# One softmax pass without the replication step, projections moved between attention blocks, and an output stage per chunk

## The chip, the cores and the metric

The kernel runs on one core of a Trainium2 chip. The metric is the device time of one execution in microseconds. Four runs of the kernel before took 351.17 to 352.73 us, with a median of 352.28 us. The profile is of one further execution, which took 352.67 us; its span, from the first to the last instruction, is 350.8 us.

## The reference

All tensors are bf16. `x` has S = 2048 rows of D = 512. Attention has 32 heads of 16 elements and a window of eight keys at distances 0, 2, ..., 14 (causal); the feed-forward part has 1792 inner columns.

```
xn  = layernorm(x)
q, k, v = split(xn @ wqkv)                      # 32 heads x 16
logit[h,s,w] = q[h,s] . k[h,s-2w] / 4           # w = 0..7, masked where s-2w < 0
o[h,s] = sum_w softmax_w(logit)[h,s,w] * v[h,s-2w]
s   = o @ wo
h   = gelu_tanh(xn @ w_gate) * (xn @ w_up)
g   = silu(h @ w_down)
out = x + s * g
```

## The kernel before

**Layout.** The sequence is worked on in four chunks of 512 columns (`CH`), and activations are transposed: a tile is 128 features by 512 positions. D is four blocks of 128 features (`NF`). `kT` and `vT` hold k and v of the whole sequence with 14 zero columns ahead, so that a window element is the same tile read `off` = 2w columns earlier. Products of positions with shifted positions are done on VectorE (`prod`, `avp`); TensorE sums them with constant matrices.

**Start (lines 65 to 146).** GpSimd and VectorE build constants: `ident`; `b56` (sums 16 rows of a head); `rep` and `summat`, each from 16 copies of 32x32 blocks on VectorE. SyncE loads `x` and `wqkv`, then the three feed-forward weights. ScalarE copies the v columns of `wqkv` into another order (`wvp`, line 122). Sixteen row tiles are normalised (VectorE and ScalarE) and transposed on TensorE into `xnT`.

**Per chunk (lines 163 to 290).** In program order:
- Projection: 12 groups of four matmuls give q, k (line 168) and v (line 181); ScalarE copies each out of PSUM (lines 177 and 187).
- Scores: 32 `prod` on VectorE (line 198) and 32 matmuls with a 128x32 stationary operand (line 202). Four window elements share one PSUM tile, each in its own 32 partitions (`L_lo`, `L_hi`).
- Softmax: two `Exp` (line 212), two `den_ps` matmuls with `summat`, `Ln` and `Exp` for the reciprocal `rden` (lines 223, 225). Eight `er_ps` matmuls with `rep` (line 229) spread each window element's 32 rows over 128, and ScalarE copies them to `erep` (line 233).
- Values: for each of four blocks, eight `avp` on VectorE (line 239), eight matmuls with `ident` into `acc` (line 243), and one product with `rden` into `oT_sb` (line 247).
- Feed-forward: for each of 14 inner blocks, eight matmuls into `g_ps` and `u_ps` (line 259); GELU by its sigmoid form in three ScalarE and three VectorE instructions (lines 266 to 277), giving `h_q`. Then for each of four row blocks 14 `dacc` matmuls (line 282), `sig` (line 287) and `g_t` (line 289); GpSimd writes `g_t` to DRAM (line 290).

**Final stage (lines 299 to 318),** after all chunks: for each of 16 row blocks four `s_ps` matmuls with `wo_sb` (line 305), a load of `g_t` back (GpSimd queue, line 311) and of `x` (SyncE queue, line 313), two VectorE products (lines 315, 317) and a store.

**Order.** A planner fixes one order for each engine ahead of the run. Mostly it is program order; an instruction whose inputs and buffers are planned to be ready is put ahead where an engine would stand idle. All PSUM tiles share one pool of eight banks. `prod` has eight buffers, `avp` four, `q_sb` two, and `h_q` one. ScalarE loads a function table where `Exp`, `Ln` or `Sigmoid` follows another of them (ACT_TABLE_LOAD).

Of the kernel before, what the change touches and what calls it, by code (L numbers as in the profile page):

```python
# [17 lines left out]
def kernel(  # L18
# [52 lines left out]
    b56f = consts.tile([P, 56], F32, name="b56f")  # L71
    nc.gpsimd.memset(b56f[:], 1.0)
    nc.gpsimd.affine_select(
        out=b56f[:], in_=b56f[:], compare_op=ALU.is_ge, fill=0.0,
        base=384, pattern=[[-16, 56]], channel_multiplier=1,
    )
    nc.gpsimd.affine_select(
        out=b56f[:], in_=b56f[:], compare_op=ALU.is_ge, fill=0.0,
        base=-369, pattern=[[16, 56]], channel_multiplier=-1,
    )  # L80
    b56 = consts.tile([P, 56], BF, name="b56")
    nc.gpsimd.tensor_copy(out=b56[:], in_=b56f[:])
    rep = consts.tile([P, 4, P], BF, name="rep")
    nc.gpsimd.memset(rep[:], 0.0)
    for wl in range(4):
        for dl in range(4):
            nc.vector.tensor_copy(
                out=rep[32 * wl:32 * wl + 32, wl, 32 * dl:32 * dl + 32],
                in_=ident[32 * wl:32 * wl + 32, 32 * wl:32 * wl + 32],
            )  # L90
    summat = consts.tile([P, P], BF, name="summat")
    for pb in range(4):
        for mb in range(4):
            nc.vector.tensor_copy(
                out=summat[32 * pb:32 * pb + 32, 32 * mb:32 * mb + 32],
                in_=ident[32 * pb:32 * pb + 32, 32 * pb:32 * pb + 32],
            )
    eps_t = consts.tile([P, 1], F32, name="eps_t")
# [11 lines left out]
    g_dram = dram.tile([S, D], BF, name="g_dram")  # L110
# [40 lines left out]
    nc.sync.dma_start(out=wd_sb[:], in_=B_w_down.rearrange("(k p) n -> p k n", p=P))  # L151
    QT = CH
    assert QT == 512 and NCK * CH == S
    with tc.tile_pool(name="prodp", bufs=8) as prodp, \
            tc.tile_pool(name="ep", bufs=2) as ep, \
# [3 lines left out]
            tc.tile_pool(name="hq", bufs=1) as hq, \  # L159
            tc.tile_pool(name="ffnp", bufs=2) as ffnp:  # L160
        for c in range(NCK):
            t0 = c * CH
            q_sb = qp.tile([P, NF, CH], BF, name="q_sb")
            for fq in range(2 * NF):
                col = fq * P
                ps = psum.tile([P, CH], F32, name="ps", tag="mm512")
                for kt in range(NKT):
                    nc.tensor.matmul(  # L168
                        ps[:], lhsT=wqkv_sb[:, kt, col:col + P],
                        rhs=xnT[:, kt, t0:t0 + CH],  # L170
                        start=(kt == 0), stop=(kt == NKT - 1),
                    )
                if fq < NF:
                    dst = q_sb[:, fq, :]
                else:
                    dst = kT[:, fq - NF, PAD + t0:PAD + t0 + CH]
                nc.scalar.activation(out=dst, in_=ps[:], func=ACT.Copy)  # L177
            for b in range(NF):
                psv = psum.tile([P, CH], F32, name="psv", tag="mm512")
                for kt in range(NKT):  # L180
                    nc.tensor.matmul(  # L181
                        psv[:], lhsT=wvp[:, kt, b * P:(b + 1) * P],
                        rhs=xnT[:, kt, t0:t0 + CH],
                        start=(kt == 0), stop=(kt == NKT - 1),
                    )
                dst = vT[:, b, PAD + t0:PAD + t0 + CH]
                nc.scalar.activation(out=dst, in_=psv[:], func=ACT.Copy)
# [31 lines left out]
            den_ps = psum.tile([P, CH], F32, name="den_ps", tag="mm512")
            nc.tensor.matmul(den_ps[:], lhsT=summat[:], rhs=e_lohi[0][:], start=True, stop=False)  # L220
            nc.tensor.matmul(den_ps[:], lhsT=summat[:], rhs=e_lohi[1][:], start=False, stop=True)
            lnd = work.tile([P, CH], F32, name="lnd", bufs=2)
            nc.scalar.activation(out=lnd[:], in_=den_ps[:], func=ACT.Ln)
            rden = work.tile([P, CH], F32, name="rden", bufs=2)
            nc.scalar.activation(out=rden[:], in_=lnd[:], func=ACT.Exp, scale=-1.0)
            erep = erepp.tile([P, W, CH], BF, name="erep")
            for w in range(W):
                er_ps = psum.tile([P, CH], F32, name="er_ps", tag="mm512")
                nc.tensor.matmul(  # L229
                    er_ps[:], lhsT=rep[:, w % 4, :], rhs=e_lohi[w // 4][:],  # L230
                    start=True, stop=True,
                )
                nc.scalar.activation(out=erep[:, w, :], in_=er_ps[:], func=ACT.Copy)  # L233
# [44 lines left out]
            for j in range(QT // P):  # L278
# [70 lines left out]
```

## Time and profile before

| what | value |
|---|---|
| median of four runs | 352.28 us |
| profiled execution: its time / its span | 352.67 us / 350.8 us |
| TensorE busy | 293.1 us (84%), 1288 matmuls |
| VectorE busy | 241.5 us (69%) |
| ScalarE busy | 195.4 us (56%) |
| GpSimd busy | 28.5 us (8%) |
| mean granted TensorE clock | 0.968 |

A busy TensorE in this table is not TensorE at its pace: a 128x512 matmul has a duration of 379 ns, but in an unbroken run the next one starts 216 ns after it, so that durations overlap. The pace is read from a run of many matmuls, less the last one's duration.

### The profile page before, as it was taken

What the parts mean: (1) busy time and instruction counts of PE and PEld (TensorE: products, weight loads), DVE (VectorE), ACT (ScalarE), POOL (GpSimd) and SP (SyncE); (2) the same over time, 40 slices, a digit from 0 to 9 for tenths busy, and PEclk for the clock granted to TensorE, in tenths of its full rate; (3) what the DMA queues carried; (4) which work ended last, traced back from release to release, by engine and by line L of the source; (5) the groups of instructions that cost most, each with busy time, mean ns of one, the idle gap of its engine ahead of it and who ended that gap; (6) DMA issues with size and microseconds to landing.
All of it is one profiled execution on the core that took longest, in us unless ns stands there. A gap on an engine that the chain in (4) does not pass through costs nothing.

```text
span 350.8 us, 3905 instructions
## 1 busy us (share of the span) xinstructions
PE 293.1 (84%) x1288; PEld 121.5 (35%) x1288; DVE 241.5 (69%) x584; ACT 195.4 (56%) x333; POOL 28.5 (8%) x69
## 2 busy tenths in 40 slices
PE   0239986999899959999899689998999599989940
PEld 0224321344344213444343224443432134434410
DVE  5971677989723959798328598995167698972764
ACT  2396663499526471897255817993465448962000
POOL 7400000000020000000110000000100100001430
PEclk9999998999999998999999989999999899999995
DMA  7992000000010000000000000000100300001685
GB/s 250 365 398 96 1 0 0 3 0 0 0 47 15 0 0 3 0 1 2 30 30 0 2 1 0 0 2 15 47 2 0 91 0 2 0 0 46 206 258 181
DMA packets 12180, 18.34 MB, mean 52 GB/s; under 512 B 1408, under 2 KB 9344, under 8 KB 12160
## 3 DMA queue, kind: packets, MB, share of 16 engines
q1 hardware_dynamic: 10112, 13.37, 10.9%
q0 software_dynamic: 2048, 4.72, 4.4%
q8 instruction: 10, 0.16, 0.2%
q14 instruction: 10, 0.08, 0.1%
HBM read 13.89 MB, written 4.19 MB: 52 GB/s over the span
## 4 chain that ended last, share of the span: by engine, by line
PE 40%; DVE 21%; issue 16%; ACT 11%; DMA 8%; POOL 1%; SPq 1%; DVEq 0%; POOLq 0%; ACTq 0%
PE ps L168 8%; DVE h_q L277 8%; PE dacc L282 7%; PE L_hi L202 5%; DVE gg_sb L276 4%; PE acc L243 4%; PE L_lo L202 4%; PE psv L181 4%; DMA wqkv_sb<-in_A_wqkv_dram 4%; DVE t_sb L270 4%; ACT sg_sb L274 3%; DVE avp L239 3%; DMA x_t<-in_A_x_dram 3%; PE g_ps L259 2%; PE er_ps L229 2%
## 5 line engine op out<-in xcount | busy, mean ns | idle before, releaser
L198 DVE TENSOR_TENSOR prod<-q_sb,kT 128x512 bf16<-128x512 bf16 x128 | 44.7, 418 | 29.0 <-ACT kT L177 23.4
L259 PE MATMUL u_ps<-xnT,wu_sb 128*128 128x512 bf16 x224 | 59.4, 379 | 0.0
L259 PE MATMUL g_ps<-xnT,wg_sb 128*128 128x512 bf16 x224 | 58.1, 379 | 0.0
L239 DVE TENSOR_TENSOR avp<-erep,vT 128x512 bf16<-128x512 bf16 x128 | 45.7, 417 | 17.6 <-ACT erep L233 17.1
L243 PE MATMUL acc<-avp,ident 128*128 128x512 bf16 x128 | 45.1, 429 | 14.8 <-DVE avp L239 14.4
L266 ACT ACTIVATE gs_sb<-g_ps 128x512 bf16<-128x512 f32 x56 | 33.4, 596 | 40.2 <-PE g_ps L259 39.5
L282 PE MATMUL dacc<-wd_sb,h_q 128*128 128x512 bf16 x224 | 50.0, 379 | 5.0 <-DVE h_q L277 5.0
L277 DVE TENSOR_TENSOR h_q<-gg_sb,u_ps 128x512 bf16<-128x512 bf16 x56 | 38.5, 687 | 5.8
L274 ACT ACTIVATE sg_sb<-t_sb 128x512 bf16<-128x512 bf16 x56 | 34.7, 630 | 11.1 <-DVE t_sb L270 11.1
L270 DVE SCALAR_TENSOR_TENSOR t_sb<-s_sb,gs_sb 128x512 bf16<-128x512 bf16 x56 | 36.7, 684 | 4.0 <-ACT s_sb L268 4.0
L268 ACT ACTIVATE s_sb<-g_ps 128x512 bf16<-128x512 f32 x56 | 33.1, 591 | 0.0
L282 PEld LDWEIGHTS <-h_q 128*128 128x128 bf16 x224 | 21.3, 98 | 33.2 <-DVE h_q L277 8.6
L259 PEld LDWEIGHTS <-wu_sb 128*128 128x128 bf16 x224 | 21.9, 98 | 26.5
L289 DVE TENSOR_TENSOR g_t<-sig,dacc 128x512 bf16<-128x512 bf16 x16 | 11.0, 687 | 29.0 <-ACT sig L287 29.0
L259 PEld LDWEIGHTS <-wg_sb 128*128 128x128 bf16 x224 | 21.9, 98 | 26.0
L168 PE MATMUL ps<-xnT,wqkv_sb 128*128 128x512 bf16 x128 | 29.8, 393 | 0.0
L290 POOL DMA_DIRECT2D g_dram<-g_t x16 | 8.7, 545 | 244.5 <-DVE g_t L289 244.5
L243 PEld LDWEIGHTS <-ident 128*128 128x128 bf16 x128 | 13.5, 106 | 43.3 <-issue 35.2
L276 DVE TENSOR_TENSOR gg_sb<-sg_sb,gs_sb 128x512 bf16<-128x512 bf16 x56 | 23.6, 422 | 6.3 <-ACT sg_sb L274 4.5
L287 ACT ACTIVATE sig<-dacc 128x512 bf16<-128x512 f32 x16 | 9.6, 597 | 32.6 <-PE dacc L282 32.6
L145 PE MATMUL psT_f<-ident,xn_t 128*128 128x128 bf16 x64 | 8.1, 311 | 20.8 <-DVE xn_t L138 19.8
L233 ACT ACTIVATE erep<-er_ps 128x512 bf16<-128x512 f32 x32 | 17.0, 593 | 8.3 <-PE er_ps L229 8.2
(56 smaller groups left out, 265.6 us busy)
## 6 DMA issues: line engine op xcount, KB each, us to landing
xg<-in_A_x_dram SPq DMA_DIRECT2D x4, 512.0 KB, 5.7
g_dram<-g_t POOLq DMA_DIRECT2D x16, 128.0 KB, 2.0
x_t<-in_A_x_dram SPq DMA_DIRECT2D x16, 128.0 KB, 3.3
g_t<-g_dram POOLq DMA_DIRECT2D x16, 128.0 KB, 3.3
out_dram<-o_t SPq DMA_DIRECT2D x16, 128.0 KB, 3.1
wg_sb<-in_B_w_gate_dram SPq DMA_DIRECT2D x1, 1792.0 KB, 17.6
wu_sb<-in_B_w_up_dram SPq DMA_DIRECT2D x1, 1792.0 KB, 20.2
wd_sb<-in_B_w_down_dram SPq DMA_DIRECT2D x1, 1792.0 KB, 23.1
```

What stands on the lines that cost most here:

```text
L168: nc.tensor.matmul(ps[:], lhsT=wqkv_sb[:, kt, col:col + P], rhs=xnT[:, kt, t0:t0 + CH], start=(kt == 0), stop=(kt == NKT - 1),)
L198: nc.vector.tensor_tensor(out=prod[:], in0=q_sb[:, f, :], in1=kT[:, f, PAD + t0 - off:PAD + t0 - off + CH], op=ALU.mult,)
L239: nc.vector.tensor_tensor(out=avp[:], in0=erep[:, w, :], in1=vT[:, b, PAD + t0 - off:PAD + t0 - off + CH], op=ALU.mult,)
L243: nc.tensor.matmul(acc[:], lhsT=ident[:], rhs=avp[:], start=(w == 0), stop=(w == W - 1),)
L259: nc.tensor.matmul(dst_ps[:], lhsT=wsb[:, kt, f * P:(f + 1) * P], rhs=xnT[:, kt, t0q:t0q + QT], start=(kt == 0), stop=(kt == NKT - 1),)
L266: nc.scalar.activation(out=gs_sb[:], in_=g_ps[:], func=ACT.Copy)
L268: nc.scalar.activation(out=s_sb[:], in_=g_ps[:], func=ACT.Square, scale=SQA)
L270: nc.vector.scalar_tensor_tensor(out=t_sb[:], in0=s_sb[:], scalar=1.0, in1=gs_sb[:], op0=ALU.add, op1=ALU.mult,)
L274: nc.scalar.activation(out=sg_sb[:], in_=t_sb[:], func=ACT.Sigmoid, scale=K2)
L276: nc.vector.tensor_tensor(out=gg_sb[:], in0=sg_sb[:], in1=gs_sb[:], op=ALU.mult)
L277: nc.vector.tensor_tensor(out=h_q[:, f, :], in0=gg_sb[:], in1=u_ps[:], op=ALU.mult)
L282: nc.tensor.matmul(dacc[:], lhsT=h_q[:, f, j * P:(j + 1) * P], rhs=wd_sb[:, f, :], start=(f == 0), stop=(f == NFF - 1),)
```

## The change

- `b56`, `rep` and `summat` are replaced by `brep`: four 128x128 matrices, each the head-sum matrix of a block repeated four times across its columns. GpSimd builds it in fp32 with 32 selects, and VectorE copies it to bf16 once.
- A score matmul uses `brep[:, f, :]` and fills all 128 rows of a PSUM tile `L_w`, one tile per window element. `Exp` writes it to `erep` directly, so that the `er_ps` matmuls and their copies go. `den_ps` is eight matmuls with `ident` over `erep`. There are eight `Exp` on a chunk's scores in place of two.
- The projection of chunk 0 is done first. That of chunk c+1 is written between the value blocks of chunk c, four groups of four matmuls behind each of the first three blocks. The product with `rden` of block b is written behind the sums of block b+1.
- The final stage is written into the feed-forward loop: behind each `dacc` row block come its `s_ps`, the load of `x`, both products and the store. `g_t` stays on the chip. `wo` is loaded on the SyncE queue behind the other weights.

```diff
-    b56f = consts.tile([P, 56], F32, name="b56f")
...
-    rep = consts.tile([P, 4, P], BF, name="rep")
...
-    summat = consts.tile([P, P], BF, name="summat")
...
+    brep_f32 = consts.tile([P, NF, P], F32, name="brep_f32")
+    nc.gpsimd.memset(brep_f32[:], 1.0)
+    for f in range(NF):
+        for dl in range(4):
+            blk = brep_f32[:, f, 32 * dl:32 * dl + 32]
+            nc.gpsimd.affine_select(out=blk, in_=blk, ...
+            nc.gpsimd.affine_select(out=blk, in_=blk, ...
+    brep = consts.tile([P, NF, P], BF, name="brep")
+    nc.vector.tensor_copy(out=brep[:], in_=brep_f32[:])
     eps_t = consts.tile([P, 1], F32, name="eps_t")
     nc.gpsimd.memset(eps_t[:], EPS)
...
     nc.sync.dma_start(out=wd_sb[:], in_=B_w_down.rearrange("(k p) n -> p k n", p=P))
+    for b in range(NF):
+        for dl in range(4):
+            d = 4 * b + dl
+            nc.sync.dma_start(out=wo_sb[32 * dl:32 * dl + 32, b, :], ...
...
+            tc.tile_pool(name="gpool", bufs=2) as gpool, \
+            tc.tile_pool(name="iop", bufs=2) as iop, \
...
+        def project(c, g, q_dst):
+            t0 = c * CH
+            ps = psum.tile([P, CH], F32, name="ps", tag="mm512")
+            for kt in range(NKT):
...
+                nc.tensor.matmul(
+                    ps[:], lhsT=wt, rhs=xnT[:, kt, t0:t0 + CH],
+                    start=(kt == 0), stop=(kt == NKT - 1),
+                )
...
+            nc.scalar.activation(out=dst, in_=ps[:], func=ACT.Copy)
+
+        q_next = qp.tile([P, NF, CH], BF, name="q_sb")
+        for g in range(3 * NF):
+            project(0, g, q_next)
         for c in range(NCK):
...
+            erep = erepp.tile([P, W, CH], BF, name="erep")
+            den_ps = psum.tile([P, CH], F32, name="den_ps", tag="mm512")
             for w in range(W):
                 off = w * DIL
+                L_w = psum.tile([P, CH], F32, name="L_w", tag="mm512")
                 for f in range(NF):
...
                     nc.tensor.matmul(
-                        Lt[32 * wl:32 * wl + 32, :],
-                        lhsT=b56[:, 24 - 8 * f:56 - 8 * f],
-                        rhs=prod[:],
+                        L_w[:], lhsT=brep[:, f, :], rhs=prod[:],
                         start=(f == 0), stop=(f == NF - 1),
-                        tile_position=(0, 32 * wl),
-                    )
...
+                nc.scalar.activation(out=erep[:, w, :], in_=L_w[:], func=ACT.Exp, scale=SCALE)
+                if c == 0 and off > 0:
+                    nc.gpsimd.memset(erep[:, w, 0:off], 0.0)
+            for w in range(W):
+                nc.tensor.matmul(
+                    den_ps[:], lhsT=ident[:], rhs=erep[:, w, :],
+                    start=(w == 0), stop=(w == W - 1),
+                )
...
-                er_ps = psum.tile([P, CH], F32, name="er_ps", tag="mm512")
...
+                accs.append(acc)
+                if b > 0:
+                    nc.vector.tensor_tensor(
+                        out=oT_sb[:, b - 1, t0:t0 + CH], in0=accs[b - 1][:], in1=rden[:], op=ALU.mult,
+                    )
+                if c + 1 < NCK and b < 3:
+                    for g in range(4 * b, 4 * b + 4):
+                        project(c + 1, g, q_next)
...
-                g_t = ffnp.tile([P, D], BF, name="g_t")
+                g_t = gpool.tile([P, D], BF, name="g_t")
                 nc.vector.tensor_tensor(out=g_t[:], in0=sig[:], in1=dacc[:], op=ALU.mult)
-                nc.gpsimd.dma_start(out=g_dram[i * P:(i + 1) * P, :], in_=g_t[:])
...
+                s_ps = psum.tile([P, D], F32, name="s_ps", tag="mm512")
...
+                x_t = iop.tile([P, D], BF, name="x_t")
+                nc.sync.dma_start(out=x_t[:], in_=xf[i * P:(i + 1) * P, :])
...
+                nc.sync.dma_start(out=of[i * P:(i + 1) * P, :], in_=o_t[:])
```

## Rows read from the trace of the kernel before

**Rows 1.** Chain of waits, the score stage's first step per chunk: start us, us, what

```profile
40.68 3.56 PE L_lo L202 x16
...
113.67 3.56 PE L_lo L202 x16
...
187.11 3.56 PE L_lo L202 x16
...
260.23 3.56 PE L_lo L202 x16
```

**Rows 2.** Busy time by stretch: us, PE, PEld, DVE, ACT, POOL (xinstructions), PEclk, DMA, GB/s

```profile
103.30:113.60 10.30, 10.30 (x49) 4.51 (x47) 3.73 (x9) 7.17 (x12) 0.54 (x1) 1.00 0.04 16
113.60:137.30 23.70, 18.88 (x68) 5.73 (x68) 18.48 (x53) 10.91 (x16) 0.00 (x0) 0.93 0.00 0
137.30:168.20 30.90, 29.64 (x138) 13.16 (x137) 26.77 (x51) 24.68 (x43) 0.00 (x0) 1.00 0.01 1
168.20:176.70 8.50, 8.50 (x40) 3.88 (x41) 2.06 (x3) 1.79 (x3) 1.63 (x3) 1.00 0.12 41
323.20:337.10 13.90, 13.90 (x65) 6.13 (x63) 9.60 (x19) 0.60 (x1) 5.48 (x10) 1.00 0.67 211
337.10:350.80 13.70, 0.03 (x1) 0.00 (x0) 7.48 (x15) 0.00 (x0) 2.19 (x4) 0.69 0.66 203
```

**Rows 3.** Timeline of TensorE, chunk 1: start us, us, instruction, [idle before]

```profile
103.15 7.07 PE L168 MATMUL ps<-xnT,wqkv_sb 128*128 128x512 bf16 x32
...
113.60 3.63 PE L202 MATMUL L_lo<-prod,b 128*32 128x512 bf16 x16
...
128.65 2.02 PE L243 MATMUL acc<-avp,ident 128*128 128x512 bf16 x5 [2.05 <-DVE avp L239]
...
137.30 0.38 PE L259 MATMUL g_ps<-xnT,wg_sb 128*128 128x512 bf16 x1
...
162.99 3.91 PE L282 MATMUL dacc<-wd_sb,h_q 128*128 128x512 bf16 x17
168.16 8.59 PE L282 MATMUL dacc<-wd_sb,h_q 128*128 128x512 bf16 x39 [1.26 <-DVE h_q L277]
```

**Rows 4.** Timeline of VectorE, chunk 1

```profile
114.03 8.14 DVE L198 TENSOR_TENSOR prod<-q_sb,kT 128x512 bf16<-128x512 bf16 x24 [1.38 <-PE L_lo L202]
...
128.17 2.07 DVE L239 TENSOR_TENSOR avp<-erep,vT 128x512 bf16<-128x512 bf16 x5 [2.00 <-ACT erep L233]
130.16 0.68 DVE L247 TENSOR_TENSOR oT_sb<-acc,rden 128x512 bf16<-128x512 f32 x1
130.76 2.79 DVE L239 TENSOR_TENSOR avp<-erep,vT 128x512 bf16<-128x512 bf16 x8
```

**Rows 5.** Timeline of ScalarE, chunk 1

```profile
123.33 1.28 ACT L223 ACT_TABLE_LOAD   x1
124.62 0.60 ACT L223 ACTIVATE lnd<-den_ps 128x512 f32<-128x512 f32 x1
```

**Rows 6.** Timelines of GpSimd, VectorE, ScalarE, TensorE, the start

```profile
1.84 0.22 POOL L73 TENSOR_SCALAR_AFFINE_SELECT b56f<-b56f 128x56 f32<-128x56 f32 x1
...
8.85 1.62 DVE L87 COPY rep<-ident 32x32 bf16<-32x32 bf16 x16
...
16.17 4.15 ACT L122 ACTIVATE wvp<-wqkv_sb 128x512 bf16<-128x512 bf16 x4 [0.63 <-DMA wqkv_sb<-in_A_wqkv_dram]
...
28.66 8.56 PE L168 MATMUL ps<-xnT,wqkv_sb 128*128 128x512 bf16 x32
```

**Rows 7.** Timelines of TensorE and VectorE, the end

```profile
323.16 13.98 PE L305 MATMUL s_ps<-wo_sb,oT_sb 128*128 128x512 bf16 x64
...
323.99 0.69 DVE L289 TENSOR_TENSOR g_t<-sig,dacc 128x512 bf16<-128x512 bf16 x1 [2.33 <-ACT sig L287]
...
347.74 0.42 DVE L317 TENSOR_TENSOR o_t<-sg,x_t 128x512 bf16<-128x512 bf16 x1 [0.16 <-DMA x_t<-in_A_x_dram]
```

**Rows 8.** DMA issues of the page: KB each, median us to landing

```profile
x_t<-in_A_x_dram SPq DMA_DIRECT2D x16, 128.0 KB, 3.3
```

More of the change, by code (lines that the diff above doesn't have):

```diff
@@ L161 @@
+        q_next = qp.tile([P, NF, CH], BF, name="q_sb")
+        for g in range(3 * NF):
+            project(0, g, q_next)
         for c in range(NCK):
             t0 = c * CH
[L163 to L187, printed above, removed]
@@ L219 @@
[L219 to L222, printed above, removed]
+                nc.scalar.activation(out=erep[:, w, :], in_=L_w[:], func=ACT.Exp, scale=SCALE)
+                if c == 0 and off > 0:
+                    nc.gpsimd.memset(erep[:, w, 0:off], 0.0)
@@ L223 @@
+            for w in range(W):
[3 more added lines that the diff above has]
+                )
+            lnd = work.tile([P, CH], F32, name="lnd", bufs=1)
             nc.scalar.activation(out=lnd[:], in_=den_ps[:], func=ACT.Ln)
-            rden = work.tile([P, CH], F32, name="rden", bufs=2)
+            rden = work.tile([P, CH], F32, name="rden", bufs=1)
             nc.scalar.activation(out=rden[:], in_=lnd[:], func=ACT.Exp, scale=-1.0)
-            erep = erepp.tile([P, W, CH], BF, name="erep")
@@ L227 @@
-            for w in range(W):
-                er_ps = psum.tile([P, CH], F32, name="er_ps", tag="mm512")
[L229 to L233, printed above, removed]
+            accs = []
             for b in range(NF):
@@ L246 @@
                     )
-                nc.vector.tensor_tensor(
-                    out=oT_sb[:, b, t0:t0 + CH], in0=acc[:], in1=rden[:], op=ALU.mult,
-                )
+                accs.append(acc)
+                if b > 0:
+                    nc.vector.tensor_tensor(
+                        out=oT_sb[:, b - 1, t0:t0 + CH], in0=accs[b - 1][:], in1=rden[:], op=ALU.mult,
+                    )
+                if c + 1 < NCK and b < 3:
+                    for g in range(4 * b, 4 * b + 4):
+                        project(c + 1, g, q_next)
+            nc.vector.tensor_tensor(
+                out=oT_sb[:, NF - 1, t0:t0 + CH], in0=accs[NF - 1][:], in1=rden[:], op=ALU.mult,
+            )
             q = c
@@ L301 @@
-    with tc.tile_pool(name="iop", bufs=3) as iop:
-        for i in range(NT):
-            s_ps = psum.tile([P, D], F32, name="s_ps", tag="mm512")
-            for b in range(NF):
-                nc.tensor.matmul(
-                    s_ps[:], lhsT=oT_sb[:, b, i * P:(i + 1) * P],
-                    rhs=wo_sb[:, b, :],
-                    start=(b == 0), stop=(b == NF - 1),
-                )
-            g_t = iop.tile([P, D], BF, name="g_t2")
-            nc.gpsimd.dma_start(out=g_t[:], in_=g_dram[i * P:(i + 1) * P, :])
-            x_t = iop.tile([P, D], BF, name="x_t")
-            nc.sync.dma_start(out=x_t[:], in_=xf[i * P:(i + 1) * P, :])
-            sg = iop.tile([P, D], BF, name="sg")
-            nc.vector.tensor_tensor(out=sg[:], in0=g_t[:], in1=s_ps[:], op=ALU.mult)
-            o_t = iop.tile([P, D], BF, name="o_t")
-            nc.vector.tensor_tensor(out=o_t[:], in0=sg[:], in1=x_t[:], op=ALU.add)
-            nc.sync.dma_start(out=of[i * P:(i + 1) * P, :], in_=o_t[:])
+                s_ps = psum.tile([P, D], F32, name="s_ps", tag="mm512")
@@ new lines @@
+                for b in range(NF):
+                    nc.tensor.matmul(
+                        s_ps[:], lhsT=oT_sb[:, b, i * P:(i + 1) * P],
+                        rhs=wo_sb[:, b, :],
+                        start=(b == 0), stop=(b == NF - 1),
+                    )
+                x_t = iop.tile([P, D], BF, name="x_t")
+                nc.sync.dma_start(out=x_t[:], in_=xf[i * P:(i + 1) * P, :])
+                sg = iop.tile([P, D], BF, name="sg")
+                nc.vector.tensor_tensor(out=sg[:], in0=g_t[:], in1=s_ps[:], op=ALU.mult)
@@ L322 @@
+                o_t = iop.tile([P, D], BF, name="o_t")
+                nc.vector.tensor_tensor(out=o_t[:], in0=sg[:], in1=x_t[:], op=ALU.add)
+                nc.sync.dma_start(out=of[i * P:(i + 1) * P, :], in_=o_t[:])
 _INS = ['A_x', 'A_wqkv', 'A_wo', 'B_x', 'B_w_gate', 'B_w_up', 'B_w_down']
```

65 lines of the change are left out of this document (22 added, 43 removed).

## The prediction

> **What bounds the kernel now.** I read the chain of waits first, for where each chunk begins; then busy time by stretch, for the engine that limits each stretch; then the timelines of one chunk, for what ends each idle time.
>
> The chain [rows 1] gives a path by stage. The start and the first projection end at 40.68 us; from score stage to score stage it is 72.99, 73.44 and 73.12; the last chunk, which has no further projection behind it, lasts 260.23 to 323.16, or 62.93; the final stage takes the rest of the 350.8 us span, 27.64. The profiled execution took 352.67 us, so 1.87 us lie around the span; it is 0.39 us above the median of the four runs (352.28).
>
> Within a chunk the limit changes. During projection and `dacc` TensorE is busy all the time; in feed-forward VectorE and ScalarE are near full too; in the scores and values (23.7 us) TensorE has 18.88 us of overlapping durations, VectorE 18.48 and ScalarE 10.91, and nobody is full [rows 2]. TensorE's pace is read from an unbroken run: 32 matmuls in 7.07 us, less the last one's 0.38, over 31, is 0.216 us each [rows 3]. A chunk has 48 + 32 + 2 + 8 + 32 + 112 + 56 = 290 of them, 62.6 us, so about 10.8 of 73.4 us are idle: 1.26 before the last `dacc` run, waiting for `h_q`, and the rest between scores and values. There VectorE waits 2.00 us for `erep` and TensorE 2.05 us for `avp` behind it [rows 3, 4]: ScalarE copies `erep` between two table loads of 1.28 us for `Ln` and `Exp` [rows 5].
>
> The final stage keeps TensorE at pace for its first half (64 matmuls in 13.98 us [rows 7]), but then nothing is left for it, and 13.7 us pass with VectorE at 7.48 us busy [rows 2], loading, multiplying and storing 16 row blocks.
>
> **The change part by part.**
>
> *TensorE's count.* The eight `er_ps` go, `den_ps` grows from two to eight, `s_ps` comes in (16): 304 per chunk with a projection inside, 65.7 us, and 256 in the last, 55.3 us. This is the floor of a chunk. That a score matmul now has 128 columns in place of 32 is costed at nothing: 16 of the old ones took 3.63 us, (3.63 - 0.38)/15 = 0.217 each, the same pace as a full one [rows 3].
> The Trainium skill (TensorE: Matmul & The Clock Gate, section Measured speedup vs the span model) says that matmuls on different column tiles run at once, three 32-column ones 2.38 times faster. By that the old form would have had something to lose: 32 x 0.216 x (1 - 1/2.38) = 4.0 us per chunk, an estimate, and a sum of 333 in place of 317. The row above shows no overlap, so there is nothing to lose.
>
> *Scores.* VectorE makes eight `prod` ahead (eight buffers); the other 24 come at (8.14 - 0.42)/23 = 0.336 us [rows 4]. Counted from T, where TensorE turns to the scores, VectorE first has `g_t`, `sg` and `o_t` of the last row block: `g_t` ends 1.52 us after its `dacc` [rows 7], which is T + 0.6, since four `s_ps` (0.86) lie between; with 0.60 for `sg` (the step from `oT_sb` to the next `avp` [rows 4], which also reads PSUM) and 0.35 for `o_t`, `prod` number nine starts at T + 1.55. The last score matmul ends at 1.55 + 24 x 0.336 + 0.3 = T + 9.9, against 6.9 us of work. Seven `den_ps` (1.5) can fill these gaps.
>
> *Values and projection.* `avp` now starts right behind the last `prod`, because `erep` comes straight from `Exp`; the wait of 2.0 us goes. Four `avp` fit their buffers, so behind each 16 projection matmuls (3.46) VectorE has only four ready; a block's eight sums then take 0.86 for these and about 1.15 for four more at 0.336, 2.0 in all. In strict program order: `den_ps` to 11.6, first block to 13.6, three times 5.5, end at T + 30.1; its 120 matmuls are 25.9, so 4.2 idle. With the planner filling gaps this goes towards 0. I take 2.7, `den_ps` alone filled, since the order before does put feed-forward matmuls between late sums (from 137.30 on [rows 3]) but not earlier ones.
>
> *Feed-forward and output.* 184 matmuls, 39.8 us, plus the 1.26 stall, kept. So 65.7 + 2.7 + 1.3 = 69.7 per chunk (67.0 to 71.2). The last chunk has no projection to cover VectorE: 32 `avp` and four `oT_sb` take 32 x 0.336 + 4 x 0.60 = 13.2 from T + 9.6, sums end at 23.1, then 41.1, less eight early feed-forward matmuls (1.7): 62.5 (56.6 to 64.2).
>
> *Covered edits.* A row block now takes 18 matmuls, 3.9 us; an `x_t` load lands in 3.3 us [rows 8] and has two buffers, so a lead of 7.8. Behind a store that waits for `o_t` on SyncE's queue stands only the `x_t` load two blocks on. Without the cover each block is late by what it misses, on SyncE and VectorE, and TensorE sees it only when banks run out. The sixteen `wo` loads go behind `wd`, some 60 us ahead of their first use. `Ln` waits for `den_ps` with the projection's copies queued behind it: two loads and two functions, about 2 x 1.28 + 2 x 0.6 = 3.8 us [rows 5]. Den and two sums leave five banks, 4.3 us of projection; without that cover TensorE would lose up to 3.8 per chunk. `rden` itself is not needed before the second block is summed. In chunk 0 seven GpSimd memsets stand between `Exp` and its readers; only the last could be late, by a fraction of a us.
>
> *Start.* VectorE loses two sets of 16 copies, 1.62 us for the `rep` set [rows 6] and as much for `summat`, of the same shape and count, and gains one copy of 128x512. GpSimd gets 32 selects of 128x32: between 0.13 (by elements) and 0.22 us (the 128x56 one [rows 6]) each, 4.1 to 7.0 us, with `eps_t`, which the first root needs, behind them: ready by about 10 us, while `xn_t` waited until 12 before. ScalarE still holds 4.15 us of `wvp` from 16.17 on, when `wqkv` lands [rows 6]. Bounds: 3.3 us earlier to 0.8 later. I take 1.2 earlier: scores at 39.5.
>
> *End.* From the last `dacc`: `g_t` ends at +1.52, `sg` 0.6, `o_t` 0.42, and from the last `o_t` (348.16) to the end of the span 2.64 us pass [rows 7]: 5.2, of which 0.86 lies beside `s_ps`. So 4.3 behind TensorE (4 to 5) replaces 27.64.
>
> *Sum.* 39.5 + 3 x 69.7 + 62.5 + 4.3 = 315.4 of span, + 1.9 around it: 317 us. Its own bounds: 37.4 + 201.0 + 56.6 + 4 + 1.9 = 301 and 41.5 + 213.6 + 64.2 + 5 + 1.9 = 326.
>
> **The rivals.**
>
> *The projection does not fill.* The planner might put the projection as one block, so that scores and values stay limited by VectorE. Then each chunk is as the last plus 10.4 of projection: 72.9; 39.5 + 218.7 + 62.5 + 4.3 + 1.9 = 327. For it: before, the projection of the next chunk, ready from the start, did not fill the 1.26 stall [rows 3]. Against: it is now written between the sums.
>
> *VectorE becomes the bound.* `prod` of the next chunk is ready during feed-forward, where VectorE is busy 26.77 of 30.9 us [rows 2] and `h_q` hangs on it. Eight of them put there cost 8 x 0.336 = 2.7 us per chunk; with the strict order, 65.7 + 4.2 + 1.3 + 2.7 = 73.9: and 64.2 + 2.7 = 66.9 for the last: 39.5 + 221.7 + 66.9 + 4.3 + 1.9 = 334. Against: `prod` comes behind all feed-forward in program order.
>
> *Table loads on ScalarE: slower.* If scores of the next chunk are planned into feed-forward, an `Exp` stands between two `Sigmoid`, with two loads of 1.28 us and 0.5 of its own, 3.07. ScalarE has 30.9 - 24.68 = 6.2 us free there [rows 2]. Eight per chunk cost 24.6 - 6.2 = 18.4, in three chunks 55: 372. It decides from six of the eight, 18.4 - 6.2 = 12.2 x 3 against a gain of 35. For it: nothing in the program forbids it. Against: the score tiles' banks come behind all `dacc` and `s_ps` tiles in one pool, and no next-chunk matmul went ahead of `dacc` before.
> The Trainium skill (ScalarE: Activation LUTs, What ACT_TABLE_LOAD costs) adds a drain of about 1380 ns to the 1283 ns of a load; it would decide from about three or four. Here `Ln` starts at 124.62, at the load's end [rows 5], so no drain is seen.
>
> **How the numbers follow.** Forecast 317 (301 to 326): 0.66. No fill, 327: 0.14. VectorE bound, 334: 0.13. Table loads, 372: 0.04. Better than 301: 0.03. The range 304 to 334 takes in the first three for the most part. A measurement of this kernel tells about 0.3%, 1.1 us, from no change: faster 0.95, same 0.01, slower 0.04.
>
> **What would show it.** Right: score stages some 70 us apart, the first at about 39 us; no wait of VectorE for `erep`; projection matmuls between the `acc` ones; the end about 4 us behind TensorE's last matmul; TensorE idle 4 us per chunk. Wrong: projections in one block; `prod` among `h_q` instructions; more than four table loads per chunk; ScalarE's copies late behind `Ln` with TensorE waiting for banks; a score matmul slower than 0.217; transposes waiting for `eps_t` or `brep`.

## The result and the profile after

The changed kernel takes 319.62 us (median of ten runs, 319.21 to 320.76) against 351.78 us for the kernel before (15 runs beside them, 349.66 to 353.92): a ratio of 0.909, 95% interval 0.907 to 0.911. The forecast was 317 us, range 304 to 334. The profiled execution took 319.56 us, its span is 317.3 us.

The page of the changed kernel: the span, busy time by engine, granted clock by slice, and the chain by engine.

```profile
span 317.3 us, 3791 instructions
...
PE 286.5 (90%) x1280; PEld 124.0 (39%) x1280; DVE 238.7 (75%) x553; ACT 191.6 (60%) x325; POOL 7.2 (2%) x49
...
PEclk9999999999999999999999999999999999999999
...
PE 75%; DVE 16%; ACT 6%; DMA 1%; issue 1%; DVEq 0%
```

TensorE's overlapping durations fill 90% of the span, not 84%, and the chain is 75% TensorE. The granted clock stays at its upper level (mean 0.999, before 0.968). An `x_t` load lands in 2.2 us (median of 16), not 3.3 [rows 8].

TensorE's timeline of the changed kernel (start us, us, instruction, idle before it); the answer to [rows 1] and [rows 3]:

```profile
39.07 8.00 PE L197 MATMUL L_w<-prod,brep 128*128 128x512 bf16 x29
...
108.56 2.35 PE L197 MATMUL L_w<-prod,brep 128*128 128x512 bf16 x10
111.20 6.41 PE L197 MATMUL L_w<-prod,brep 128*128 128x512 bf16 x19 [0.29 <-DVE prod L193]
...
118.34 0.38 PE L197 MATMUL L_w<-prod,brep 128*128 128x512 bf16 x1
118.56 1.46 PE L205 MATMUL den_ps<-erep,ident 128*128 128x512 bf16 x6
119.85 1.68 PE L223 MATMUL acc<-avp,ident 128*128 128x512 bf16 x6
121.36 0.38 PE L166 MATMUL ps<-xnT,wqkv_sb 128*128 128x512 bf16 x1
121.58 0.62 PE L223 MATMUL acc<-avp,ident 128*128 128x512 bf16 x2
122.03 3.40 PE L166 MATMUL ps<-xnT,wqkv_sb 128*128 128x512 bf16 x15
...
137.63 0.62 PE L223 MATMUL acc<-avp,ident 128*128 128x512 bf16 x2
...
165.15 0.39 PE L270 MATMUL dacc<-wd_sb,h_q 128*128 128x512 bf16 x1 [0.35 <-DVE h_q L265]
...
167.67 2.98 PE L270 MATMUL dacc<-wd_sb,h_q 128*128 128x512 bf16 x13 [0.83 <-DVE h_q L265]
...
179.12 2.35 PE L197 MATMUL L_w<-prod,brep 128*128 128x512 bf16 x10
...
249.67 2.35 PE L197 MATMUL L_w<-prod,brep 128*128 128x512 bf16 x10
```

Score stages start at 39.07, 108.56, 179.12 and 249.67: chunks of 69.5, 70.6 and 70.6 us, where they were 73.0 to 73.4 [rows 1]. In chunk 1 the scores last from T = 108.56 to T + 10.0: the first ten matmuls go at TensorE's pace, and from 111.20 on they start (6.41 - 0.38)/18 = 0.335 us apart, which is the pace of `prod` on VectorE. The sums end at 138.09, T + 29.5. Projection (`ps`) stands between the sums, but six sums go ahead of it and two behind its first matmul in each block: `avp` has four buffers. The two waits for `h_q` before the late `dacc` runs are 0.35 and 0.83 us, counted from the end of the matmul before.

VectorE's timeline of chunk 1; the answer to [rows 4]:

```profile
110.73 7.46 DVE L193 TENSOR_TENSOR prod<-q_sb,kT 128x512 bf16<-128x512 bf16 x22
...
120.34 2.77 DVE L219 TENSOR_TENSOR avp<-erep,vT 128x512 bf16<-128x512 bf16 x8 [0.80 <-PE acc L223]
...
125.69 2.77 DVE L219 TENSOR_TENSOR avp<-erep,vT 128x512 bf16<-128x512 bf16 x8 [1.76 <-PE acc L223]
...
134.33 1.75 DVE L193 TENSOR_TENSOR prod<-q_sb,kT 128x512 bf16<-128x512 bf16 x5
```

The 2.00 us wait for `erep` is gone. In its place stand 0.80 and 1.76 us for `acc`, that is, for an `avp` buffer that TensorE frees late. Eight `prod` of the next chunk run inside the sums, the last five of them at 134.33. Of this chunk's other 24 `prod`, two run between `g_t`, `sg` and `o_t` of the last row block, and 22 follow from 110.73 to T + 9.63 without idle time.

ScalarE in chunk 1; the answer to [rows 5]:

```profile
119.37 1.28 ACT L210 ACT_TABLE_LOAD   x1
120.67 0.60 ACT L210 ACTIVATE lnd<-den_ps 128x512 f32<-128x512 f32 x1
...
123.11 1.23 ACT L176 ACTIVATE q_sb<-ps 128x512 bf16<-128x512 f32 x2
```

The load and `Ln` are as before; what now stands behind them, and behind the load and `Exp` for `rden`, is the projection's first copy, at 123.11.

GpSimd, VectorE, ScalarE and TensorE at the start; the answer to [rows 6]:

```profile
1.74 0.86 POOL L76 TENSOR_SCALAR_AFFINE_SELECT brep_f<-brep_f 128x32 f32<-128x32 f32 x5
...
6.64 0.10 POOL L87 MEMSET eps_t<- 128x1 f32 x1
...
13.73 4.16 ACT L109 ACTIVATE wvp<-wqkv_sb 128x512 bf16<-128x512 bf16 x4
...
27.39 8.39 PE L166 MATMUL ps<-xnT,wqkv_sb 128*128 128x512 bf16 x32
```

The selects run 0.16 us apart, `eps_t` is there by 6.7 us, and `wvp` starts at 13.73 right behind two `xnT` copies, where it had waited for `wqkv` until 16.17; the projection starts at 27.39, not 28.66. The load of `wqkv` (KB, us to landing), before and after:

```profile
wqkv_sb<-in_A_wqkv_dram SPq DMA_DIRECT2D x1, 1536.0 KB, 13.2
...
wqkv_sb<-in_A_wqkv_dram SPq DMA_DIRECT2D x1, 1536.0 KB, 10.5
```

The end, TensorE and VectorE; the answer to [rows 7]:

```profile
312.00 1.03 PE L280 MATMUL s_ps<-wo_sb,oT_sb 128*128 128x512 bf16 x4
...
314.34 0.42 DVE L290 TENSOR_TENSOR o_t<-sg,x_t 128x512 bf16<-128x512 bf16 x1
```

From the last `s_ps` run's end at TensorE's pace (312.00 + 4 x 0.216 = 312.86) to the end of the span are 4.4 us; after the last `dacc` there had been a final stage of 27.64, half of it with TensorE idle [rows 2].

| term | forecast | measured |
|---|---|---|
| first score matmul | 39.5 | 39.07 |
| three chunks | 209.1 | 69.49 + 70.56 + 70.55 = 210.6 |
| last chunk, to TensorE's end | 62.5 | 312.86 - 249.67 = 63.2 |
| behind TensorE | 4.3 | 4.4 |
| around the span | 1.9 | 319.56 - 317.3 = 2.3 |
| sum | 317.3 | 319.6 |

### The profile page after: what moved, and what is told of

The parts are those of the page before. It is cut to its first block, busy times and chain, and to the rows that moved or that the text cites. A ratio compares the mean times of both kernels' runs of the same rounds, so it can differ in the third digit from the quotient of the medians.

```text
span 317.3 us, 3791 instructions
## 1 busy us (share of the span) xinstructions
PE 286.5 (90%) x1280; PEld 124.0 (39%) x1280; DVE 238.7 (75%) x553; ACT 191.6 (60%) x325; POOL 7.2 (2%) x49
## 4 chain that ended last, share of the span: by engine, by line
PE 75%; DVE 16%; ACT 6%; DMA 1%; issue 1%; DVEq 0%
PE g_ps L247 14%; PE ps L166 13%; PE u_ps L247 13%; PE dacc L270 11%; PE L_w L197 9%; PE acc L223 8%; DVE h_q L265 4%; PE s_ps L280 2%; PE den_ps L205 2%; DVE stats L118 2%; DVE avp L219 2%; ACT xnT L133 2%; DVE gg_sb L264 2%; ACT sg_sb L262 2%; DVE t_sb L258 2%; ACT wvp L109 1%
## 5 line engine op out<-in xcount | busy, mean ns | idle before, releaser
L247 PE MATMUL u_ps<-xnT,wu_sb 128*128 128x512 bf16 x224 | 57.5, 379 | 0.0
L270 PE MATMUL dacc<-wd_sb,h_q 128*128 128x512 bf16 x224 | 52.3, 379 | 4.7 <-DVE h_q L265 4.6
L219 DVE TENSOR_TENSOR avp<-erep,vT 128x512 bf16<-128x512 bf16 x128 | 44.6, 418 | 9.5 <-PE acc L223 9.4
L197 PE MATMUL L_w<-prod,brep 128*128 128x512 bf16 x128 | 38.3, 378 | 0.9 <-DVE prod L193 0.9
L223 PE MATMUL acc<-avp,ident 128*128 128x512 bf16 x128 | 37.3, 378 | 1.1 <-DVE avp L219 1.1
L275 ACT ACTIVATE sig<-dacc 128x512 bf16<-128x512 f32 x16 | 9.6, 597 | 41.4 <-PE dacc L270 41.4
L166 PE MATMUL ps<-xnT,wqkv_sb 128*128 128x512 bf16 x128 | 31.0, 391 | 0.0
L201 ACT ACTIVATE erep<-L_w 128x512 bf16<-128x512 f32 x32 | 18.7, 597 | 16.5 <-PE L_w L197 16.3
L197 PEld LDWEIGHTS <-brep 128*128 128x128 bf16 x128 | 12.1, 97 | 24.8 <-issue 15.5
## 6 DMA issues: line engine op xcount, KB each, us to landing
wqkv_sb<-in_A_wqkv_dram SPq DMA_DIRECT2D x1, 1536.0 KB, 10.5
```

The source lines that it names most:

```text
L166: nc.tensor.matmul(ps[:], lhsT=wt, rhs=xnT[:, kt, t0:t0 + CH], start=(kt == 0), stop=(kt == NKT - 1),)
L197: nc.tensor.matmul(L_w[:], lhsT=brep[:, f, :], rhs=prod[:], start=(f == 0), stop=(f == NF - 1),)
L219: nc.vector.tensor_tensor(out=avp[:], in0=erep[:, w, :], in1=vT[:, b, PAD + t0 - off:PAD + t0 - off + CH], op=ALU.mult,)
L223: nc.tensor.matmul(acc[:], lhsT=ident[:], rhs=avp[:], start=(w == 0), stop=(w == W - 1),)
L247: nc.tensor.matmul(dst_ps[:], lhsT=wsb[:, kt, f * P:(f + 1) * P], rhs=xnT[:, kt, t0q:t0q + QT], start=(kt == 0), stop=(kt == NKT - 1),)
L270: nc.tensor.matmul(dacc[:], lhsT=h_q[:, f, j * P:(j + 1) * P], rhs=wd_sb[:, f, :], start=(f == 0), stop=(f == NFF - 1),)
```

## The experiments

Times are medians; ratios are to the kernel before, run beside each. "L_w starts" are the starts of the score stages.

### Each part alone

The kernel before with the output stage in the loop (and the `wo` loads moved behind the weights), nothing else:

```diff
-                nc.gpsimd.dma_start(out=g_dram[i * P:(i + 1) * P, :], in_=g_t[:])
+                s_ps = psum.tile([P, D], F32, name="s_ps", tag="mm512")
...
+                nc.sync.dma_start(out=of[i * P:(i + 1) * P, :], in_=o_t[:])
```

> The kernel before with the output stage alone moved into the feed-forward loop (wo on SyncE, no trip through DRAM; lnd, rden, g_t and sg have one buffer to make room). My theory: the 27.64 us of the final stage become 64 matmuls of 0.216 us inside the chunks (13.8) and 4.3 behind the last one, so 9.5 us less: 342 us, 339 to 344. Rival (the output stage carries most of the 32 us, the rest is small): 325 us or less.

Measured: 342.14 us (341.49 to 342.75), ratio 0.975 [0.971, 0.978]: 9.1 us, where 9.5 were worked out; the scores start at 39.61.

The kernel before with `brep`, `L_w`, eight `Exp` and the new `den_ps` alone:

```diff
-                        Lt[32 * wl:32 * wl + 32, :],
-                        lhsT=b56[:, 24 - 8 * f:56 - 8 * f],
...
+                        L_w[:], lhsT=brep[:, f, :],
```

> The kernel before with the softmax part alone changed (brep, Exp straight to erep, no er_ps); the projection stays ahead of the scores and the final stage stays at the end. My theory: from the first score matmul T the scores end at T + 8.5 (24 prod behind eight ready ones), the sums at T + 21.7 (32 avp and four oT_sb on VectorE), against T + 26.9 before; 5 us less per chunk and 1.3 at the start: 330.5 us, 327 to 335. Rival (only the count of matmuls matters, two fewer per chunk): 349 to 351 us.

Measured: 339.65 us (338.24 to 340.02), ratio 0.966 [0.962, 0.970]: 11.6 us, about nine less than expected. L_w starts 41.42, 111.30, 181.39, 251.25: 69.9 per chunk, a gain of 3.2 where 5 was expected, and a start 0.8 later where 1.3 earlier was expected. VectorE's timeline of this kernel in chunk 1 shows two of the waits that were not counted:

```profile
122.00 2.10 DVE L209 TENSOR_TENSOR avp<-erep,vT 128x512 bf16<-128x512 bf16 x6 [0.80 <-PE acc L213]
124.90 0.69 DVE L217 TENSOR_TENSOR oT_sb<-acc,rden 128x512 bf16<-128x512 f32 x1 [0.80 <-ACT rden L203]
```

With no projection between the sums VectorE waits for the first `acc` behind eight `den_ps`, then 0.80 for `rden`. The start is answered by the chain: the longest piece in it is the landing of `wqkv`, 13.39 us, with the 16 `wo` loads still issued beside it; `wvp` waits 2.4 us for it.

The changed kernel with each chunk's projection as one block ahead of its scores:

```diff
-                if c + 1 < NCK and b < 3:
-                    for g in range(4 * b, 4 * b + 4):
-                        project(c + 1, g, q_next)
...
+            for g in range(3 * NF):
+                project(c, g, q_sb)
```

> The changed kernel with the projection of a chunk as one block at that chunk's start, as before; softmax and output stay changed. As the prediction had it in its rival, 327 us: the projections between the sums are worth 7 to 8. Worked out again from the trace after: a chunk is 10.4 of projection, 21.7 of scores and values and 39.4 of feed-forward and output, 71.5 against 70.2 measured, so the interleaving is worth only 1 to 2 us in each of three chunks: 322 to 324 us. Rival (it costs more than it gives): 319 or less.

Measured: 326.63 us (325.10 to 326.89), ratio 0.929 [0.926, 0.933]. TensorE's timeline, the projection blocks:

```profile
101.89 7.07 PE L166 MATMUL ps<-xnT,wqkv_sb 128*128 128x512 bf16 x32
...
174.73 7.07 PE L166 MATMUL ps<-xnT,wqkv_sb 128*128 128x512 bf16 x32
...
247.22 7.07 PE L166 MATMUL ps<-xnT,wqkv_sb 128*128 128x512 bf16 x32
```

They start 72.8 and 72.5 apart. So the places of the projection are worth 7.0 us. The first rival (72.9 per chunk, 327) put the right price on this form; the expectation reworked before the run (322 to 324) was too low.

Alone the first two parts give 9.1 and 11.6; the third, taken out of the whole, costs 7.0. The whole gives 32.2, 4.5 more than these add up to. About 1.3 of it is the start: from 40.61 before, the first part alone moves it 1.0 earlier (39.61), the second 0.8 later (41.42), and both together 1.5 earlier (39.07). The rest was not traced.

### What a wider score matmul costs

The kernel before with its score matmuls reading `q_sb` directly (the products with k are left out), so that nothing feeds them late; `L_lo` with neighbours on different column tiles (32 of TensorE's 128 columns each), `L_hi` with four in a row on the same:

```diff
+            for f in range(NF):
+                for wl in range(4):
+                    nc.tensor.matmul(
+                        L_lo[32 * wl:32 * wl + 32, :],
...
+                        rhs=q_sb[:, f, :],
```

> The disputed cost by itself. The kernel before without the prod products (the score matmuls read q directly, so the logits are left out), so that nothing but TensorE paces the score matmuls. L_lo is summed with neighbouring matmuls on different column tiles (32 columns each), L_hi with four in a row on the same column tile, as before. My theory from the trace of before (no overlap): both 16-runs start a matmul every 0.216 us, 3.5 us each. Rival, the Trainium skill (TensorE: Matmul & The Clock Gate, Measured speedup vs the span model): different column tiles run at once, so the L_lo run takes less than half of the L_hi run, 1.5 us or less; then widening to 128 columns gave up something that the order before had not used.

Measured: 335.84 us (one run). TensorE's timeline of both runs of 16, of the first four matmuls of each, and ScalarE's `Exp` of `L_hi` (granted clock 1.00 here):

```profile
110.47 1.05 PE L193 MATMUL L_lo<-q_sb,b 128*32 128x512 bf16 x16
111.34 1.07 PE L202 MATMUL L_hi<-q_sb,b 128*32 128x512 bf16 x16
...
110.47 0.40 PE L193 MATMUL L_lo<-q_sb,b 128*32 128x512 bf16 x4
...
111.34 0.42 PE L202 MATMUL L_hi<-q_sb,b 128*32 128x512 bf16 x4
...
112.98 0.59 ACT L212 ACTIVATE e_t<-L_hi 128x512 bf16<-128x512 f32 x1
```

Sixteen take (111.34 - 110.47)/16 = 0.054 us each, four in the time of one full matmul, in either order. They go in fours: four start within 0.04 us, and the next four 0.22 us after them. `Exp` reads `L_hi` at 112.98, so the sums were indeed done by then; at 0.216 each `L_hi` would have taken until 114.8. So matmuls on different column tiles run side by side, and the 0.217 of [rows 3] was not TensorE's pace. The trace doesn't name the tile of a matmul: whether the planner or TensorE brought the four of `L_hi` together, where the program has four in a row on one tile, stays open.

TensorE's timeline of `L_lo` in the kernel before shows what the 0.217 was. Its first two, first eight and last eight matmuls:

```profile
113.60 0.40 PE L202 MATMUL L_lo<-prod,b 128*32 128x512 bf16 x2
...
113.60 1.05 PE L202 MATMUL L_lo<-prod,b 128*32 128x512 bf16 x8
...
114.51 2.72 PE L202 MATMUL L_lo<-prod,b 128*32 128x512 bf16 x8
```

The eight `prod` made ahead belong to two window elements, so to two tiles, and their matmuls go in pairs: the eighth starts 0.67 us after the first, where at 0.216 it would be 1.5. The other eight start 0.335 us apart, as VectorE makes `prod` [rows 4]. That is (0.91 + 7 x 0.335)/15 = 0.217 on average, equal to TensorE's 0.216 by coincidence.

The changed kernel with three of four score matmuls narrowed again:

```diff
+                    n = P if f == 0 else 32
...
-                        L_w[:], lhsT=brep[:, f, :], rhs=prod[:],
...
+                        L_w[0:n, :], lhsT=brep[:, f, 0:n], rhs=prod[:],
```

> The changed kernel in which the score matmuls of f = 1 to 3 write 32 partitions, not 128 (their sums for the other 96 partitions are left out, so the output is not the reference's); f = 0 stays whole. 24 matmuls of 32 go from 0.216 us to about 0.06. Theory (in the changed kernel VectorE paces the scores, so the widening that costs TensorE about 0.155 us x 32 = 5 us per chunk is covered there): 319 to 320.5 us, the last of a chunk's score matmuls still 10 us after the first. Rival (TensorE's time in the scores is on the path): 24 x 0.155 = 3.7 us less per chunk, 319.6 - 15 = 305 us, or 308 where half a chunk's is hidden.

Measured: 321.71 us (321.43 to 322.09), ratio 0.914 [0.911, 0.916]: nothing gained, and 1.2 us above the theory's bound; chunks are 71.0 us. But this run doesn't decide between the two, because the narrowed matmuls did not get faster: all of them write the same first 32 partitions, so they share one column tile. TensorE's timeline, three of them whose `prod` lie ready, then a change of width:

```profile
109.80 0.82 PE L198 MATMUL L_w<-prod,brep 128*32 128x512 bf16 x3
...
118.40 0.38 PE L206 MATMUL den_ps<-erep,ident 128*128 128x512 bf16 x1
118.70 0.60 PE L198 MATMUL L_w<-prod,brep 128*32 128x512 bf16 x2
```

The three start (0.82 - 0.38)/2 = 0.22 us apart, as full ones do, not 0.06. A matmul that follows one of another width starts 0.30 to 0.33 later, not 0.22. The last score matmul starts 0.3 later after its `prod` than in the changed kernel, and the last six `den_ps` at T + 10.4, not T + 10.0; that is the 0.4 by which a chunk is longer.

That VectorE, not TensorE, paces the scores of the changed kernel is shown by other rows. Its `prod` run without idle time and end at T + 9.63, and 19 of the 32 score matmuls start at their pace of 0.335. With twice the `prod` buffers (below) the same wide matmuls end at T + 7.2. So the widening's 5 us per chunk, 32 x (0.216 - 0.054), lie beside VectorE. Narrow score matmuls on four tiles in the changed kernel were not run.

### What covers the Ln chain

The changed kernel with two more one-column functions between `Ln` and `rden`, which cost two more table loads, about 3.0 us, ahead of the projection's copies:

```diff
+            nc.scalar.activation(out=xtra[:], in_=lnd[:, 0:1], func=ACT.Sigmoid)
+            nc.scalar.activation(out=xtra[:], in_=xtra[:], func=ACT.Ln)
```

> The changed kernel with two more function-table loads between Ln and the Exp that gives rden: a Sigmoid and an Ln of one column each, about 3.0 us more on ScalarE in each chunk, with the projection's copies queued behind them. As the prediction had it, five free banks give 4.3 us of room against 3.8 used, so 0.5 of the 3.0 is covered and 2.5 per chunk is lost in three chunks: 327 us. Rival (the chain is covered more deeply, since TensorE has sums to do between the projection groups): 319 to 321 us.

Measured: 319.96 us (319.84 to 320.39), ratio 0.912 [0.910, 0.914]; L_w starts 108.44, 179.01, 249.58, the same 70.6. ScalarE's timeline of it:

```profile
123.97 0.63 ACT L215 ACTIVATE rden<-lnd 128x512 f32<-128x512 f32 x1
...
126.02 2.04 ACT L176 ACTIVATE q_sb<-ps 128x512 bf16<-128x512 f32 x4
```

The first `q_sb` copy starts at T + 17.6 (126.02), not T + 14.6 (123.11), TensorE's order does not change, and only the first `oT_sb` product waits (1.64 us for `rden`) in time that VectorE otherwise spent waiting for `acc`. The cover is 3.8 + 3.0 = 6.8 us at least, not 4.3. The timeline of the changed kernel has block 0's eight sums between the last `den_ps` and most of the projection (119.85 to 122.03), and block 1's eight behind its first four groups; the count of five banks left both out.

### Where the idle 4.9 us of a chunk are

A chunk of 70.55 has 65.7 us of matmuls. Scores and values hold 29.5 - 121 x 0.216 = 3.4 idle (one gate matmul stands among the last sums). From the first `dacc` at 162.04 to the next scores 72 matmuls take 17.1, so 1.5 is idle there; the 0.35 and 0.83 for `h_q` are counted from the end of a matmul, and the next could have started 0.16 before that end. Four kernels each take one wait (the first two with one `erep` buffer, to make room):

```diff
-    with tc.tile_pool(name="prodp", bufs=8) as prodp, \
+    with tc.tile_pool(name="prodp", bufs=16) as prodp, \
```

> The changed kernel with sixteen prod buffers in place of eight (erep has one buffer to make room). Theory: what is left of idle time between a chunk's first score matmul and its den_ps is VectorE's 24 prod at 0.336 behind sg and o_t; with sixteen made ahead only 16 are left, so scores end at T + 7.2 in place of T + 10.0, 2.8 less in each of chunks 1 to 3: 311 us, up to 314 if the prod made ahead hold up h_q. Rival (TensorE is the bound of the chunk already, or another wait is right behind): 318 to 320.

Measured: 314.27 us (314.08 to 315.69), ratio 0.895 [0.893, 0.897], 69.15 per chunk. TensorE's timeline:

```profile
110.02 7.39 PE L197 MATMUL L_w<-prod,brep 128*128 128x512 bf16 x32
...
118.97 1.68 PE L223 MATMUL acc<-avp,ident 128*128 128x512 bf16 x6
...
164.51 0.39 PE L270 MATMUL dacc<-wd_sb,h_q 128*128 128x512 bf16 x1 [0.65 <-DVE h_q L265]
165.64 0.39 PE L270 MATMUL dacc<-wd_sb,h_q 128*128 128x512 bf16 x1 [0.74 <-DVE h_q L265]
...
168.15 2.55 PE L270 MATMUL dacc<-wd_sb,h_q 128*128 128x512 bf16 x11 [0.40 <-DVE h_q L265]
```

The 32 score matmuls run at TensorE's pace and end at T + 7.2, 2.8 earlier. At the end of the chunk 1.4 of it is left. `den_ps` has no gaps to fill any more, so the sums start 2.3 earlier (118.97 - 110.02 = 8.95, not 11.29). They end 2.0 earlier, with one more gate matmul among them, so 0.2 is lost there: four `avp` buffers hold them up as before, and more `prod` stand among them. Some `prod` now stand around the first `t_sb` and push `h_q` back, whose waits grow from two to three and from 1.2 to 0.65 + 0.74 + 0.40 = 1.8; from the first `dacc` to the next scores 72 matmuls take 17.84, not 17.08, so 0.8 is lost there.

```diff
-            tc.tile_pool(name="avpp", bufs=4) as avpp, \
+            tc.tile_pool(name="avpp", bufs=8) as avpp, \
```

> The changed kernel with eight avp buffers in place of four (erep has one). The prediction took VectorE's four buffers to cost about 1.15 us per block behind each group of projections. The trace after has only about 0.9 us of idle time of TensorE in the whole stretch of sums and projections, so by it 0.3 to 0.9 us per chunk: 317 to 319 us. By the prediction's strict order: four blocks at about 0.3 to 1.1 each, up to 2.7 per chunk: 312 us.

Measured: 316.93 us (315.37 to 318.35), ratio 0.903 [0.900, 0.905], 69.8 per chunk: eight sums and 16 projection matmuls alternate without a gap.

```diff
+            s_early = [out_proj(c * TPC + j) for j in range(3)]
             for j in range(QT // P):
...
+                s_ps = s_early[j] if j < 3 else out_proj(i)
```

> The changed kernel with the s_ps runs of row blocks 0 to 2 written ahead of the chunk's first dacc run, so that their twelve matmuls stand where TensorE waits for the last h_q block (0.36 + 0.83 us in chunk 1 of the changed kernel). Theory (the stall is TensorE's own time, and the scores that follow still end 10 us after their start, because the tail of the chunk with block 3's s_ps, sg and o_t is unchanged): 1.2 us goes from each of the four chunks, 319.6 - 4.8 = 315 us, range 314 to 316.5, chunks of 69.3 us. Rival (VectorE is what paces a chunk, so TensorE reaches the scores earlier and waits for prod there): 319 to 320 us, chunks of 70.5 us.

Measured: 314.61 us (314.36 to 315.18), ratio 0.894 [0.891, 0.896], 69.3 per chunk: twelve `s_ps` matmuls fill the wait, and `dacc` runs 56 in a row.

The last chunk's first six gate/up blocks between its value blocks:

```diff
+                elif b < 3:
+                    for f in range(2 * b, 2 * b + 2):
+                        gate_up(c, f, h_q)
...
```

> The changed kernel with the last chunk's gate and up blocks 0 to 5 written between its value blocks (two behind each of the first three), where the other chunks have the projection. Theory: in the last chunk VectorE is the bound from the first score to the last h_q (32 prod, 32 avp, four oT_sb and 14 blocks of three instructions, whatever their order), so TensorE's idle time there is only moved: 318 to 320 us. Rival (TensorE's idle time in the sums of the last chunk, about 4.6 us that nothing fills, is on the path): 315 us.

Measured: 318.33 us (317.46 to 318.87), ratio 0.907 [0.904, 0.909]: 1.3 us, of about 4.6 idle. From 264.84 to 299.16, the value blocks behind the first and the feed-forward, VectorE is busy for 32.1 of 34.3 us. So VectorE, not the order of TensorE's work, is the main limit of the last chunk.

### Together

16 `prod`, eight `avp`, the early `s_ps`, one `erep` and `oT_sb` per chunk:

> The changed kernel with 16 prod buffers, 8 avp buffers, the s_ps of row blocks 0 to 2 ahead of the dacc runs, and to make room one erep buffer and an oT_sb of one chunk (two buffers). Theory (three waits of TensorE at three places of a chunk, for prod, for avp and for h_q, so their gains add except where VectorE becomes the bound): alone 16 prods gave -5.4 us, 8 avp -2.7, the early s_ps is expected to give -4.8; the sum 319.6 - 12.9 = 306.7, range 306 to 310, chunks of 67.5 us. Rival (VectorE, at 239 of 317 us busy, runs out of slack: what it does ahead in the sums is taken from the avp there, and the gains overlap): 311 to 314 us, no better than the 16 prods alone.

Measured: 302.95 us (302.52 to 303.78), ratio 0.861 [0.858, 0.863], better than the range. TensorE's timeline:

```profile
106.78 7.39 PE L207 MATMUL L_w<-prod,brep 128*128 128x512 bf16 x32
...
115.73 1.89 PE L234 MATMUL acc<-avp,ident 128*128 128x512 bf16 x8
...
157.17 2.75 PE L181 MATMUL s_ps<-wo_sb,oT_sb 128*128 128x512 bf16 x12
159.76 12.49 PE L282 MATMUL dacc<-wd_sb,h_q 128*128 128x512 bf16 x56
```

66.2 per chunk, against 65.7 of matmuls. Alone the three gave 5.4 + 2.7 + 5.0 = 13.1, together 16.7. Chunks 1 and 2 are 4.4 shorter (70.55 to 66.17), where alone the three make them 1.4, 0.7 and 1.3 shorter. The run with 16 `prod` says where most of the rest was: it lost 0.2 per chunk in the sums and 0.8 at `h_q`, and now eight `avp` free the one and twelve `s_ps` (2.6 us) cover the other, about 1.0 in each of the first three chunks. The last chunk, 63.2 to 58.1, gained 0.35 more than the three alone.

With the last chunk's fill as well:

> The kernel of the combined run with gate/up blocks 0 to 5 of the last chunk written between its value blocks, where no projection of a next chunk stands. Theory (the last chunk's sums are paced by VectorE's avp; the fill moves TensorE's work into their gaps, but VectorE also has the blocks' t_sb, gg_sb and h_q to do in the same stretch): 0 to 2 us less than the combined kernel. Rival (the fill takes TensorE's 10 us of last-chunk work wholly into the gaps): 4 us less or more.

Measured: 301.24 us (300.00 to 301.84), ratio 0.855 [0.852, 0.857], another 1.7 us. This is the best version: 18 us ahead of the changed kernel.

## Why the prediction was right, step by step

- **TensorE's count as the floor, 65.7 per chunk:** right. The combined kernel comes to 66.2.
- **The wider score matmul at nothing:** the cost was right here and its reason was wrong. The step read 0.217 us in [rows 3] as TensorE's pace and rejected the page's rule by it. The Trainium skill (TensorE: Matmul & The Clock Gate, section Measured speedup vs the span model) was right that matmuls on different column tiles overlap; here it was four in the time of one. The old form did have about 32 x (0.216 - 0.054) = 5 us per chunk to lose. It could not use them, since VectorE's `prod` set the pace, behind the first eight score matmuls before and behind the first ten after, which is why the 333 by that rule did not come. That the changed kernel loses nothing rests on its timeline and on the run with 16 `prod`; the narrowed run did not make the matmuls faster and proves nothing here.
- **Scores end at T + 9.9:** measured T + 10.0. The order on VectorE differs a little (two `prod` go between `g_t`, `sg` and `o_t`), the sum does not.
- **Values and projection:** strict order was worked out as T + 30.1 with 4.2 idle, and 2.7 was taken because `den_ps` would fill gaps in the scores. Two of eight `den_ps` did; nearly the strict order came, T + 29.5 with 3.4 idle. This and the last chunk are most of the 2.3 us by which the sum was low.
- **`h_q` wait of 1.26 kept:** 0.35 + 0.83 = 1.2 as the profile counts it, 1.5 by TensorE's pace. It is real time of TensorE: the early `s_ps` gave back 5.0 us over four chunks.
- **Cover of the `Ln` chain, 4.3 against 3.8 us:** the count of five banks was too small a cover, because it left out the 16 sums around the first four projection groups. Another 3.0 us were put in and nothing was lost.
- **Last chunk 62.5:** 63.2, paced in the main by VectorE, as the small gain of the fill (1.3 us) shows.
- **Start 1.2 earlier:** 1.5 earlier, but the removed copies alone would not have done it. With the copies gone and the `wo` loads left in place the start is 41.4; with the copies left and the `wo` loads moved it is 39.6. `wqkv` lands sooner, in 10.5 us in both kernels with the `wo` loads moved, in 13.2 and 13.4 in the two without: `wvp`, which needs it, starts at 13.73, not 16.17 [rows 6], and at 16.35 where only the copies went. The 0.5 us between 39.6 and 39.07 may be the copies, but variants of the changed kernel that share its start begin their scores anywhere from 38.94 to 40.62, so it is not shown. The prediction looked at the `wo` loads' new queue, not at what they had run beside. The selects took 32 x 0.16 = 5.3 us, inside the 4.1 to 7.0, and `eps_t` was ready at 6.7.
- **End 4.3 behind TensorE:** 4.4. The output part gave 9.1 us alone.
- **Rivals:** "the projection does not fill" did not happen, but its price holds (326.6 against 327). "VectorE becomes the bound" did not: `prod` of the next chunk fell into the sums, where VectorE waited anyway, not among `h_q`. With 16 buffers some of them did fall there, at 0.8 us per chunk. No `Exp` came between `Sigmoid`; table loads stayed four per chunk.

## What to carry to other kernels

The mean pace of a run of instructions is the engine's own only if nothing fed it late: cut the run into parts, or take the feeder's pace beside it, before a rule is rejected by it. A run that is to price an operation has first to be read for whether the operation itself got cheaper in it: the narrowed score matmuls did not. Waits at several places of one loop can be one slack passed on: here removing one showed 1.4 of 2.8 us, and removing three gave more than their sum. A load that is moved is to be priced by what it ran beside in its old place as well as by its new queue.

## What the runs showed of the hardware

Matmuls of 128x512 with a 128x32 stationary operand went four at a time where they were spread over four column tiles and nothing fed them late: 0.054 us each on average, against 0.216 for 128x128, also where the program has four in a row on one tile. Those that all used the same 32 columns started 0.22 us apart, no faster than a full one. A change between the two widths cost about 0.1 us each time (0.30 to 0.33 from start to start, in place of 0.22). A load of 1536 KB landed in 13.2 to 13.4 us with sixteen loads of 32 KB on GpSimd's queue beside it, and in 10.5 us with those moved behind it.
